# Attention, a wide gated layer and eight experts on one core: a new order for the first phase, and copies by halves where the experts begin

## The chip, the cores and the metric

The kernel runs on one core of a Trainium2 chip. The metric is the device time of one execution in microseconds (us), given as the median of several runs. Of the engines, PE multiplies matrices, DVE and ACT do elementwise work, POOL does the indirect transfers and some small fills, and SP issues almost all other transfers. Each engine works through its own instructions strictly in the order in which they were emitted, so one instruction that waits holds all behind it.

## The reference, cut to what matters

Windowed attention (window 64) feeds a wide layer, and that feeds a top-1 mixture of eight experts; every token is either routed or passed through.

```python
scores = (q @ k.T) / sqrt(64), masked to 0 <= i - j < 64          # 4 x 8 heads, 576 positions, 64 wide
x = softmax(scores) @ v  -> rows of 512                            # 2304 tokens x 512
h = x @ w_in; g = h * tanh(softplus(h)); x = g @ w_out             # 512 -> 2048 -> 512
do = x @ w_skip > 0; e = argmax(x @ w_gate); p = softmax prob of e # router, 8 experts
out = x;  out[do] = x + p * (relu(x @ w1[e]) @ w2[e])              # 512 -> 1024 -> 512
```

## The kernel before, in words

The 2304 tokens are cut into six blocks of 384. In the first phase each block goes through attention (four pairs of heads, `pr`, two units each), then through the wide layer in 16 chunks of 128 hidden columns, chunk `c` being `L1` (into the chunk), an elementwise chain on DVE and ACT, and `L2` (out of it, accumulated over the block in three PSUM tiles `po`). Products are made from a high and a low part of each operand (three matmuls for one), so each weight is loaded (`wl`), put together from its words and split into two parts by DVE and ACT (`we`, `wa`, `wo`, `ws`, `wH`, `wL`) before its first use.

Nothing of this order is written by hand. Each step is a task of a list scheduler (`Plan`, lines 51 to 157): it has one or two engines with a cost, the tasks it comes `after`, the buffers it needs (`get`) and frees (`use`), a due time, and for a transfer a time `lat` from the end of its issue until its data can be used. `order` repeatedly takes, on the engine that can start first, the startable task that is due first; due times are shifted by kind of task (`LATE`), and where two engines could do a task, prices (`PRICE0` up to a planned time `TW0`, then `PRICE`, from `TW` on `PRICE2`) decide. `emit` then issues all tasks in planned order, so each engine's queue is fixed at build time. `T0`, `D0`, `D1`, `US` and `UO` set the planned times of chunks and units.

Where PE has a planned gap, `keep_warm` (line 1163) puts filler matmuls called `warm` into it, as many as fill a share `FILL` = 0.8 of the gap at 0.056 us each. This holds from the start up to the first `L2`, and again from the second routing transpose of the last block on.

In attention, `load_nat` (`lqk`, lines 414 to 427) loads the queries `nq` and keys `nk` of a pair into four shared buffers `rk`; PE transposes them (`nat_T`, `nT`), `kT` and `qT` copy them out of PSUM, `att_S` (`S`) makes the scores, `mx`, `ex`, `ep`, `rc`, `nm` the softmax, `PT` transposes the probabilities, `PV` multiplies by `v`. The scores of pair 2 must come after the `PT` of units 0 and 1, those of pair 3 after the `PT` of units 2 and 3. `lqk` is planned with `lat=2.3`.

The change to the experts, called the handover here, comes after the last chunk. For each of the three tiles `t` of the last block: `xe` copies `po` to `xs`, `rT` transposes it, `re` copies that out, `rl` multiplies by the router's weights, and a chain of tiny DVE steps finds the expert and the slot (`m1`, `su`, `fi`, `m2`, `oh`, then `pl` on PE, then `pi`, `ro`, `ke`); beside it run the gate (`se` on ACT, then `sm`, `ep`, `ga`, `tg`), the slot as an integer (`sl`) and the running count (`co`). `pm` then makes a 0/1 matrix that picks the tile's tokens for expert 0, and `se2` (`select`, line 1096) adds these tokens into two PSUM tiles `sel` by eight matmuls for each `t`: expert 0 so gets its tokens without going through memory. `xgH` copies each `sel` out, and `E1` (line 1217) starts expert 0. `sH` and `sL` split the tokens into parts for `se2`. `eH` and `eL` split weights of the first experts as their places come free.

Of the kernel before, what the change touches and what calls it, by code (L numbers as in the profile page):

```python
# [26 lines left out]
T0, D0, D1, US, UO, WO, LO = 20.57, 3.54, 4.21, 1.68, 5.52, 2.09, 3.4  # L27
# [138 lines left out]
LATE = dict(wl=-9.64, wa=-0.1, wo=-3.47, ws=-4.07, wH=-11.22, lqk=-4.23, nT=-11.43, S=-14.23, ex=-0.53, nm=-4.0, PT=0.94, Pe=7.68, xH=-13.18, L1=2.57, L2=0.89, me=1.15, n=-4.49, mn=-0.61, ln=-5.67, r=-7.61, g=3.04, gH=3.02, xe=2.94, rT=1.62, re=-6.31, rl=2.98, rs=-1.25, lg=13.87, ro=-1.68, eH=16.04, rc=1.8, PV=-0.21, wL=2.42, ga=-3.86, sL=-1.97, xo=13.29, eL=4.54, m2=6.01, bl=18.08, wb=-0.93, ke=-20.26, m1=16.67, se2=-11.46, sl=7.64, el=-0.26, qT=2.69, fz=-9.43, bt=-20.62, se=-13.56, sH=11.09, sd=-1.3, wg=-1.88, tg=9.05, fs=-2.81, xgH=-0.09, sm=9.36, oh=-8.74, su=7.71, xL=-4.21, we=3.45, pl=-8.44, gL=2.75, pi=-2.04, co=-1.2, pm=-0.37, dm=8.62, kT=-2.92, fi=-2.37, mx=3.12, L2t=14.66, ep=-14.67, rq=0.13, lv=-0.43)  # L166
# [5 lines left out]
def tile_kernel(  # L172
# [408 lines left out]
    for pr in range(NU // 2):  # L581
        t = unit_time(2 * pr) - 5
        if pr < NPE:
            T(("lqk", pr), one(SS, 1.8 if len(runs(pr // 4)) == 1 else 2.3), lambda e, pr=pr: load_nat(pr), lat=2.3,
              get=[("rk", ("nq", pr)), ("rk", ("nk", pr))], due=t, t0=.7)
# [249 lines left out]

    def x_store(m, t):
        n = 3 * m + t
        SP.dma_start(out=out[128 * n:128 * n + 128, :], in_=xs_t[m, t][:, :DM])
# [6 lines left out]
    def route_Te(eng, m, t):  # L845
# [5 lines left out]
        xf_t[m, t] = xf  # L851

# [26 lines left out]
    class Group:  # L879


        def __init__(self, m, t0, n):
            self.m, self.t0, self.n, self.i = m, t0, n, 3 * m + t0
# [113 lines left out]
    for m in range(NB):  # L997
# [3 lines left out]
        for t in range(3):  # L1001
            T(("xe", m, t), two(.48, .6), lambda e, m=m, t=t: x_evac(e, m, t), after=[("L2t", NF * m + NF - 1, t) if last else ("L2", NF * m + NF - 1)],
              get=[("xs", ("xs", m, t))], use=[("po", m, t)], due=tb + 2)
            T(("xo", m, t), one(SS, .45), lambda e, m=m, t=t: x_store(m, t), after=[("xe", m, t)], lat=2.5,
              due=tb + 20, use=[("xs", m, t)])
            T(("rT", m, t), one(PP, .43), lambda e, m=m, t=t: route_T(m, t), after=[("xe", m, t)] + [("re", m, t - 1)] * (t > 0),
              get=[("ps", ("rtp", m, t))], due=tb + dt * (2 + 2 * t), use=[("xs", m, t)])
            T(("re", m, t), two(.48, .6), lambda e, m=m, t=t: route_Te(e, m, t), after=[("rT", m, t)],
              get=[("rk" if last else "xf", ("xf", m, t))], use=[("rtp", m, t)])
# [6 lines left out]
            T(("rl", m, t), one(PP, .75), lambda e, m=m, t=t: route_lg(m, t), after=[("re", m, t), ("wg",)],  # L1016
# [5 lines left out]
        prev = None  # L1022
        for t0, n in ([(t, 1) for t in range(3)] if last else [(0, 3)]):
            g = Group(m, t0, n)
# [6 lines left out]
            def R(name, eng, cost, fn, after, use=(), late=0.0, get=(), lat=None, g=g, gb=gb, td=td):  # L1031
# [10 lines left out]
            R("pl", PP, .1, Group.place, [key("oh")] + ([prev("co")] if prev else [("co", m - 1, 0)] if m else []),  # L1042
              get=[("ps", ("pp", m, t0))])
# [8 lines left out]
            R("co", VV, .21 * n, Group.count, [key("pl")], (), 1)  # L1052
# [61 lines left out]
    for t in range(3):  # L1114
        T(("sH", t), two(.52, .34), lambda e, t=t: xs_H(e, t), after=[("xe", L, t)],
          get=[("xHL", "xsHL")] if t == 0 else (), use=[("xs", L, t)], due=te + 10 + t, behind=[("sH", t - 1)] * (t > 0))
        T(("sL", t), one(VV, .6), lambda e, t=t: xs_L(e, t), after=[("sH", t)], use=[("xs", L, t)],
# [6 lines left out]
    for i in range(2):  # L1124
        T(("xgH", i), two(.52, .6), lambda e, i=i: sel_H(e, i), after=[("se2", t, i) for t in range(3)],
          get=[("xHL", "xg0")] if i == 0 else (), use=[("sel", i)], due=te + 16, behind=[("xgH", 0)] * i)
# [6 lines left out]
    for n in range(32):  # L1133
# [8 lines left out]
        T(("eH", key), two(.52, .34), lambda e, key=key, i=i: expert_H(e, key, i), after=[("el", key), last_use[i]],  # L1142
# [21 lines left out]
    def keep_warm(key, t0, t1):  # L1164
# [5 lines left out]
        n = int((t1 - t0 - GAP) * FILL / (0.056 if t0 else 0.085))  # L1170
# [46 lines left out]
    def E1(e, fp):  # L1217
        ph_t[e, fp] = ph = pl1.tile([128, 2, N1], F32, tag="ph2", name="ph2")
        for i in range(2):
            f = 2 * fp + i  # L1220
            for kk in range(NK):
                PE.matmul(ph[:, i], w1_t[e, kk][:, 128 * f:128 * f + 128], xgT[e][:, kk, :N1],  # L1222
                          start=kk == 0, stop=kk == NK - 1)
# [242 lines left out]
```

## Time and profile before

| | us |
|---|---|
| median of 3 runs (lowest, highest) | 687.76 (687.21, 689.37) |
| the profiled execution | 687.16 |
| its span, first to last instruction | 685.4 |
| PE busy in the span | 670.7 |
| DVE busy | 460.1 |
| ACT busy | 405.6 |

PE's busy time holds the fillers too, so a share of 98% doesn't say that it does useful work for 98% of the time. Shares of an engine have to be read stage by stage, since the stages have different limits. A row of the timeline gives the start, the duration, engine, line, operation and output from inputs; a number in square brackets is how long the engine sat idle just before it, with what ended that.

### The profile page before, as it was taken

What the parts mean: (1) busy time and instruction counts of PE and PEld (TensorE: products, weight loads), DVE (VectorE), ACT (ScalarE), POOL (GpSimd) and SP (SyncE); (2) the same over time, 40 slices, a digit from 0 to 9 for tenths busy, and PEclk for the clock granted to TensorE, in tenths of its full rate; (3) what the DMA queues carried; (4) which work ended last, traced back from release to release, by engine and by line L of the source; (5) the groups of instructions that cost most, each with busy time, mean ns of one, the idle gap of its engine ahead of it and who ended that gap; (6) DMA issues with size and microseconds to landing.
All of it is one profiled execution on the core that took longest, in us unless ns stands there. A gap on an engine that the chain in (4) does not pass through costs nothing. (4 is left out here: it accounts for less than half of the span.)

```text
span 685.4 us, 13449 instructions
## 1 busy us (share of the span) xinstructions
PE 670.7 (98%) x4870; PEld 576.7 (84%) x4870; DVE 460.1 (67%) x1298; ACT 405.6 (59%) x994; POOL 55.6 (8%) x114
## 2 busy tenths in 40 slices
PE   8999999999999999999999999999999999999995
PEld 7777767788888888888888888888889888998983
DVE  5999999876665556556776656566678574685352
ACT  5888777677667676676555565455544253543241
POOL 3000000000020001000020001000020122211111
PEclk9999999999999999999999999999999999999998
DMA  9999966776432312232311100044464677578300
GB/s 199 279 316 324 248 134 141 191 162 146 77 75 47 83 35 53 47 93 50 66 44 24 47 1 16 12 153 146 147 200 146 224 251 261 200 286 300 132 27 19
DMA packets 150493, 92.54 MB, mean 135 GB/s; under 512 B 111869, under 2 KB 128253, under 8 KB 150416
## 3 DMA queue, kind: packets, MB, share of 16 engines
q1 hardware_dynamic: 147696, 87.11, 46.5%
q0 software_dynamic: 2720, 4.42, 1.8%
q8 instruction: 46, 0.75, 0.5%
q14 instruction: 31, 0.25, 0.1%
HBM read 73.96 MB, written 17.86 MB: 134 GB/s over the span
## 5 line engine op out<-in xcount | busy, mean ns | idle before, releaser
L737 PE MATMUL ph<-xH,w 128*128 128x384 f32 x768 | 221.1, 349 | 0.1
L788 PE MATMUL po<-w,gH 128*128 128x512 f32 x480 | 154.4, 403 | 0.0
L737 PEld LDWEIGHTS ph<-xH,w 128*128 128x128 f32 x768 | 141.0, 188 | 6.1 <-issue 1.9
L737 PE MATMUL ph<-xL,w 128*128 128x384 f32 x384 | 130.1, 339 | 0.0
L745 ACT ACTIVATE u<-u 128x384 f32<-128x384 f32 x96 | 50.3, 524 | 121.5 <-DVE u L742 121.5
L788 PEld LDWEIGHTS po<-w,gH 128*128 128x128 f32 x480 | 87.3, 189 | 17.1 <-issue 1.6
L788 PE MATMUL po<-w,gL 128*128 128x512 f32 x240 | 95.0, 396 | 0.0
L764 DVE SCALAR_TENSOR_TENSOR u<-u,ph 128x384 f32<-128x384 f32 x80 | 44.1, 551 | 67.7 <-ACT u L758 67.3
L737 PEld LDWEIGHTS ph<-xL,w 128*128 128x128 f32 x384 | 72.3, 188 | 4.4 <-issue 2.6
L1222 PEld LDWEIGHTS ph<-xgT,w 128*128 128x128 f32 x512 | 63.9, 190 | 1.5 <-DVE xgT L319 0.4
L1222 PE MATMUL ph<-xgT,w 128*128 128x144 f32 x512 | 64.7, 287 | 0.4 <-DVE xgT L319 0.3
L742 DVE TENSOR_SCALAR u<-ph 128x384 f32<-128x384 f32 x96 | 53.2, 554 | 15.0 <-PE ph L737 13.8
L773 DVE TENSOR_TENSOR gL<-u,gH 128x384 fp32r<-128x384 f32 x80 | 44.5, 557 | 17.1 <-ACT gH L317 14.2
L531 ACT ACTIVATE P<-P,mx 128x128 f32<-128x128 f32 x144 | 55.8, 391 | 0.3 <-DVE mx L524 0.2
L788 PEld LDWEIGHTS po<-w,gL 128*128 128x128 f32 x240 | 45.1, 188 | 10.7
L749 ACT ACTIVATE u<-u 128x384 f32<-128x384 f32 x96 | 50.4, 525 | 2.9
L755 ACT ACTIVATE u<-u 128x384 f32<-128x384 f32 x96 | 50.2, 523 | 2.3
L758 ACT ACTIVATE u<-u 128x384 f32<-128x384 f32 x96 | 50.2, 523 | 2.3
L788 PE MATMUL po<-w,g 128*128 128x512 f32 x96 | 44.0, 594 | 0.0
L343 DVE TENSOR_TENSOR w<-st,w 128x512 fp32r<-128x512 f32 x64 | 42.6, 683 | 0.6
L1266 PE MATMUL po<-w,hH 128*128 128x512 f32 x128 | 42.6, 414 | 0.0
L1249 ACT ACTIVATE hH<-ph 128x288 fp32r<-128x288 f32 x31 | 12.7, 411 | 42.8 <-PE ph L1222 42.8
(166 smaller groups left out, 965.8 us busy)
## 6 DMA issues: line engine op xcount, KB each, us to landing
st<-in_moe_w_dram SPq DMA_DIRECT2D x64, 256.0 KB, 6.0
w<-in_moe_w_dram SPq DMA_DIRECT2D x32, 512.0 KB, 5.3
w<-in_moe_w_in_dram SPq DMA_DIRECT2D x16, 512.0 KB, 6.4
w<-in_moe_w_out_dram SPq DMA_DIRECT2D x16, 512.0 KB, 6.0
out_dram<-xs SPq DMA_DIRECT2D x18, 256.0 KB, 2.4
xg<-xg_d SPq DMA_DIRECT2D x16, 257.0 KB, 4.5
ca<-w SPq DMA_DIRECT2D x16, 256.0 KB, 3.2
xg_d<-nothing SPq DMA_DIRECT2D x16, 256.0 KB, 4.8
```

The source lines that it names most:

```text
L343: eng.tensor_tensor(l, raw_w.pop(key), h.bitcast(F32), op=ALU.subtract)
L531: A.activation(P[:, i], P[:, i], AF.Exp, bias=mx[:, 0, u % 2, i:i + 1], scale=-1.0, accum_out=mx[:, 1, u % 2, i:i + 1])
L737: PE.matmul(phs[c], a[:, kk], b[:, kk], start=kk == 0 and n == 0, stop=kk == NK - 1 and n == len(terms) - 1)
L742: V.tensor_scalar(u, phs[c], 20.0, None, op0=ALU.min)
L745: A.activation(us[c], us[c], AF.Exp)
L749: A.activation(us[c], us[c], AF.Square, bias=1.0)
L755: A.activation(us[c], us[c], AF.Ln, scale=0.5, bias=half_t[c])
L758: A.activation(us[c], us[c], AF.Exp, scale=-1.0)
L764: V.scalar_tensor_tensor(o, us[c], 1.0, phs[c], op0=ALU.subtract, op1=ALU.mult)
L773: eng.tensor_tensor(gL, us[c], gH.bitcast(F32), op=ALU.subtract)
L788: PE.matmul(po[m, t], a[:, ts], b, start=f == 0 and n == 0, stop=f == NF - 1 and n == len(terms) - 1)
L1222: PE.matmul(ph[:, i], w1_t[e, kk][:, 128 * f:128 * f + 128], xgT[e][:, kk, :N1], start=kk == 0, stop=kk == NK - 1)
```

## The change

**The plan of the first phase.** `lqk` is planned with `lat` 4.8 for pairs 2 and 3 and 2.5 for the others, instead of 2.3 for all. A set of the planner's constants moves: chunk 0 is planned 0.73 earlier, the later attention units 0.62 later in all, `we` and `kT` are due earlier (by 0.90 and 0.61), the prices of the start end at a planned 23.99 instead of 30.94. All tasks of the first phase stay the same, only their order (and, where two engines are possible, the engine) is worked out anew. (Of the `LATE` table the diff below shows the changed entries alone.)

**The handover.** For the last tile (`t` = 2) `xe` and `re` are each done by halves of 256 columns, one on DVE and one on ACT. `pl` of a tile no longer waits for the running count of the tile before, but adds the one-hot rows of the tiles before it by matmuls of its own. `sl`, `sm` and `co` (and with them the gate's chain) come only after the last `pm`. The `sL` of tiles 1 and 2 come after `xe` and `re` of tile 2. The two last expert weights, (2, 5) and (2, 7), are split only after `xgH`. The two `xgH` go to ACT and DVE, one each, and are due 24 earlier. The fillers of this stage fill the whole planned gap instead of 0.8 of it. The first step of `E1` takes the halves of its sum in the order in which the two `xgH` deliver them.

```diff
-T0, D0, D1, US, UO, WO, LO = 20.57, 3.54, 4.21, 1.68, 5.52, 2.09, 3.4
+T0, D0, D1, US, UO, WO, LO = 19.84, 3.52, 4.21, 1.68, 6.87, 2.09, 3.4
-TW0 = 30.94
-PRICE0 = dict(P=0.0, V=2.28, A=0.5, G=-0.5, S=0.0)
-TW = 309.39
-PRICE2 = dict(P=0.0, V=1.26, A=2.91, G=0.0, S=0.0)
+TW0 = 23.99
+PRICE0 = dict(P=0.0, V=2.59, A=0.5, G=-0.5, S=0.0)
+TW = 319.85
+PRICE2 = dict(P=0.0, V=1.11, A=4.08, G=0.0, S=0.0)
...
-LATE: lqk=-4.23, xe=2.94, rT=1.62, rc=1.8, xo=13.29, fz=-9.43, sd=-1.3, xgH=-0.09, we=3.45, co=-1.2, kT=-2.92, fi=-2.37
+LATE: lqk=-3.93, xe=4.36, rT=1.11, rc=1.49, xo=11.62, fz=-9.66, sd=-3.55, xgH=1.14, we=2.55, co=1.72, kT=-3.53, fi=6.04
...
-            T(("lqk", pr), ..., lambda e, pr=pr: load_nat(pr), lat=2.3,
+            T(("lqk", pr), ..., lambda e, pr=pr: load_nat(pr), lat=4.8 if pr in (2, 3) else 2.5,
...
+    def x_evac_half(eng, m, t, n):
+        ...
+        hs = slice(256 * n, 256 * n + 256)
+        if eng is A:
+            A.activation(xs_t[m, t][:, hs], po[m, t][:, hs], AF.Copy, scale=-1.0)
+        else:
+            V.tensor_scalar(xs_t[m, t][:, hs], po[m, t][:, hs], -1.0, None, op0=ALU.mult)
...
+    def route_Te_half(eng, m, t, n):
+        ...
+        copy(eng, xf[:, 2 * n:2 * n + 2], p[:, 2 * n:2 * n + 2])
...
+    def front(self):
+        return self.prev.front + [self.prev.oh[:, 0]] if self.prev else []
...
-                for t2 in range(t):
-                    PE.matmul(pp[:, t], ones8, self.oh[:, t2], start=False, stop=False)
+                for o in self.front + [self.oh[:, t2] for t2 in range(t)]:
+                    PE.matmul(pp[:, t], ones8, o, start=False, stop=False)
...
-            R("pl", ..., [key("oh")] + ([prev("co")] if prev else [("co", m - 1, 0)] if m else []),
+            R("pl", ..., [key("oh")] + ([prev("oh")] if prev else [("co", m - 1, 0)] if m else []),
...
-            R("sl", VV, .07, Group.slot, [key("ro")], (), .5)
+            R("sl", VV, .07, Group.slot, [key("ro")] + [("pm", 2)] * last, (), .5)
+            calm = [("pm", 2)] * last
-            R("sm", VV, .1, Group.sum, [key("se")], (), .5)
+            R("sm", VV, .1, Group.sum, [key("se")] + calm, (), .5)
-            R("co", VV, .21 * n, Group.count, [key("pl")], (), 1)
+            R("co", VV, .21 * n, Group.count, [key("pl")] + calm + ([prev("co")] if prev else []) + [("pl", m, 2)] * last, (), 1)
...
-        T(("sL", t), one(VV, .6), ..., after=[("sH", t)], ...)
+        T(("sL", t), one(VV, .6), ..., after=[("sH", t)] + [("xe", L, 2)] * (t == 1) + [("re", L, 2)] * (t == 2), ...)
...
-        T(("xgH", i), two(.52, .6), ..., due=te + 16, behind=[("xgH", 0)] * i)
+        T(("xgH", i), one(VV if i else AA, .55), ..., due=te - 8, behind=[("xgH", 0)] * i)
...
-        T(("eH", key), two(.52, .34), ..., after=[("el", key), last_use[i]], ...)
+        T(("eH", key), two(.52, .34), ..., after=[("el", key), last_use[i]] + [("xgH", 0), ("xgH", 1)] * (key in ((2, 5), (2, 7))), ...)
...
-        n = int((t1 - t0 - GAP) * FILL / (0.056 if t0 else 0.085))
+        n = int((t1 - t0 - GAP) * (1.0 if stage[0] else FILL) / (0.056 if t0 else 0.085))
...
-            for kk in range(NK):
-                PE.matmul(ph[:, i], ..., start=kk == 0, stop=kk == NK - 1)
+        if e == 0 and fp == 0:
+            order = [(i, kk) for k2 in (0, 2) for i in range(2) for kk in (k2, k2 + 1)]
+        ...
+        for i, kk in order:
+                PE.matmul(ph[:, i], ..., start=(i, kk) == order[0], stop=(i, kk) == order[-1])
```

## Rows read from the trace of the kernel before

**Rows 1.** Windows: start:end, length, busy us (instructions) by engine, clock, DMA share, GB/s.
```profile
6.00:46.00 40.00, 35.58 (x525) 31.27 (x523) 35.16 (x129) 32.29 (x107) 2.35 (x18) 1.00 1.14 268
50.00:110.00 60.00, 60.00 (x373) 42.59 (x373) 59.21 (x153) 47.98 (x120) 1.40 (x6) 1.00 0.88 226
523.90:527.50 3.60, 3.60 (x37) 3.58 (x35) 3.52 (x17) 2.02 (x5) 0.00 (x0) 1.00 0.39 148
527.50:529.50 2.00, 2.00 (x28) 2.00 (x27) 1.72 (x20) 0.21 (x1) 0.00 (x0) 0.60 0.00 0
529.50:532.00 2.50, 2.50 (x18) 2.41 (x16) 2.08 (x19) 0.00 (x0) 0.98 (x1) 0.64 0.03 7
```

**Rows 2.** Windows of the fillers' line alone: length, PE and weight loads, clock, DMA.
```profile
6.00:46.00 40.00, 11.50 (x171) 10.12 (x168) 1.00 1.14 268
523.90:534.32 10.42, 3.19 (x32) 2.65 (x32) 0.84 0.22 83
```

**Rows 3.** Waits of DVE from 6 to 46: total us, times, longest.
```profile
DVE cv L652 <- DMA w<-in_moe_w_in_dram: 1.9, 2, 1.3
DVE cv L652 <- DMA w<-in_moe_w_out_dram: 0.7, 1, 0.7
```

**Rows 4.** Timeline of PE, first phase: pairs 2 and 3.
```profile
13.01 0.52 PE L437 MATMUL tqk<-ident,nq 96*128 96x96 f32 x4 [0.50 <-DMA nq<-in_q_dram]
...
15.37 0.99 PE L552 MATMUL tp<-ident,P 128*128 128x128 f32 x6 [0.89 <-DVE P L547]
...
16.80 1.15 PE L508 MATMUL sc<-kT,qT 64*64 64x128 f32 x24
...
20.36 0.98 PE L552 MATMUL tp<-ident,P 128*128 128x128 f32 x6
...
22.16 0.89 PE L508 MATMUL sc<-kT,qT 64*64 64x128 f32 x24
```

**Rows 5.** Timeline of DVE, first phase.
```profile
14.34 0.43 DVE L652 TENSOR_SCALAR cv<-w 128x512 int32<-128x512 int32 x1 [1.27 <-DMA w<-in_moe_w_in_dram]
```

**Rows 6.** Timeline of SP, first phase.
```profile
7.91 0.85 SPq L425 DMA_DIRECT2D nq<-in_q_dram  x1
```

**Rows 7.** Timeline of PE, handover.
```profile
525.59 1.91 PE L873 MATMUL lp<-wgs,xf 128*128 128x9 f32 x16
...
527.57 1.71 PE L1176 MATMUL warm<-ones 128*128 128x128 bf16 x17
...
529.52 0.56 PE L1099 MATMUL sel<-pick,xsH 128*128 128x256 f32 x1
...
532.44 0.56 PE L1176 MATMUL warm<-ones 128*128 128x128 bf16 x7
532.81 0.37 PE L1099 MATMUL sel<-pick,xsH 128*128 128x256 f32 x1
...
534.32 8.22 PE L1222 MATMUL ph<-xgT,w 128*128 128x144 f32 x64 [0.29 <-DVE xgT L319]
```

**Rows 8.** Timeline of DVE, handover.
```profile
524.95 0.68 DVE L343 TENSOR_TENSOR w<-st,w 128x512 fp32r<-128x512 f32 x1
525.55 0.16 DVE L898 TENSOR_REDUCE r_mx<-lp 128x1 f32<-128x8 f32 x1
...
528.71 0.34 DVE L1093 TENSOR_SCALAR pick<-iota,row_all 128x256 fp32r<-128x256 int16 x1
...
531.35 0.68 DVE L343 TENSOR_TENSOR w<-st,w 128x512 fp32r<-128x512 f32 x1
531.94 0.35 DVE L1093 TENSOR_SCALAR pick<-iota,row_all 128x256 fp32r<-128x256 int16 x1
533.58 1.29 DVE L319 COPY xgT<-sel 128x512 f32<-128x512 f32 x2 [1.29 <-PE sel L1099]
```

**Rows 9.** Groups of ACT by shape: instructions, busy us, mean ns, idle before.
```profile
L317 ACT ACTIVATE kT<-tqk 128x256 f32<-128x256 f32 x2 | 0.8, 378 | 0.2 <-PE tqk L437 0.2
L317 ACT ACTIVATE xf<-rtp 128x512 f32<-128x512 f32 x3 | 1.8, 591 | 5.1 <-PE rtp L843 5.1
```

More of the change, by code (lines that the diff above doesn't have):

```diff
@@ L583, in tile_kernel @@
         if pr < NPE:
-            T(("lqk", pr), one(SS, 1.8 if len(runs(pr // 4)) == 1 else 2.3), lambda e, pr=pr: load_nat(pr), lat=2.3,
+            T(("lqk", pr), one(SS, 1.8 if len(runs(pr // 4)) == 1 else 2.3), lambda e, pr=pr: load_nat(pr), lat=4.8 if pr in (2, 3) else 2.5,
               get=[("rk", ("nq", pr)), ("rk", ("nk", pr))], due=t, t0=.7)
@@ L1001, in tile_kernel @@
         for t in range(3):
-            T(("xe", m, t), two(.48, .6), lambda e, m=m, t=t: x_evac(e, m, t), after=[("L2t", NF * m + NF - 1, t) if last else ("L2", NF * m + NF - 1)],
-              get=[("xs", ("xs", m, t))], use=[("po", m, t)], due=tb + 2)
-            T(("xo", m, t), one(SS, .45), lambda e, m=m, t=t: x_store(m, t), after=[("xe", m, t)], lat=2.5,
+            halves = last and t == 2
+            done = [("L2t", NF * m + NF - 1, t) if last else ("L2", NF * m + NF - 1)]
+            if halves:
+                T(("xe", m, t), one(VV, .3), lambda e, m=m, t=t: x_evac_half(e, m, t, 0), after=done,
+                  get=[("xs", ("xs", m, t))], use=[("po", m, t)], due=tb + 2)
+                T(("xe2", m, t), one(AA, .3), lambda e, m=m, t=t: x_evac_half(e, m, t, 1), after=done,
+                  behind=[("xe", m, t)], use=[("po", m, t)], due=tb + 2)
+            else:
+                T(("xe", m, t), two(.48, .6), lambda e, m=m, t=t: x_evac(e, m, t), after=done,
+                  get=[("xs", ("xs", m, t))], use=[("po", m, t)], due=tb + 2)
@@ L1005, in tile_kernel @@
+            xe = [("xe", m, t)] + [("xe2", m, t)] * halves
+            T(("xo", m, t), one(SS, .45), lambda e, m=m, t=t: x_store(m, t), after=xe, lat=2.5,
               due=tb + 20, use=[("xs", m, t)])
-            T(("rT", m, t), one(PP, .43), lambda e, m=m, t=t: route_T(m, t), after=[("xe", m, t)] + [("re", m, t - 1)] * (t > 0),
+            T(("rT", m, t), one(PP, .43), lambda e, m=m, t=t: route_T(m, t), after=xe + [("re", m, t - 1)] * (t > 0),
               get=[("ps", ("rtp", m, t))], due=tb + dt * (2 + 2 * t), use=[("xs", m, t)])
-            T(("re", m, t), two(.48, .6), lambda e, m=m, t=t: route_Te(e, m, t), after=[("rT", m, t)],
-              get=[("rk" if last else "xf", ("xf", m, t))], use=[("rtp", m, t)])
+            if halves:
+                T(("re", m, t), one(VV, .3), lambda e, m=m, t=t: route_Te_half(e, m, t, 0), after=[("rT", m, t)],
+                  get=[("rk", ("xf", m, t))], use=[("rtp", m, t)])
+                T(("re2", m, t), one(AA, .3), lambda e, m=m, t=t: route_Te_half(e, m, t, 1), after=[("rT", m, t)],
+                  behind=[("re", m, t)], use=[("rtp", m, t)])
+            else:
+                T(("re", m, t), two(.48, .6), lambda e, m=m, t=t: route_Te(e, m, t), after=[("rT", m, t)],
+                  get=[("rk" if last else "xf", ("xf", m, t))], use=[("rtp", m, t)])
@@ L1124, in tile_kernel @@
     for i in range(2):
-        T(("xgH", i), two(.52, .6), lambda e, i=i: sel_H(e, i), after=[("se2", t, i) for t in range(3)],
-          get=[("xHL", "xg0")] if i == 0 else (), use=[("sel", i)], due=te + 16, behind=[("xgH", 0)] * i)
+        T(("xgH", i), one(VV if i else AA, .55), lambda e, i=i: sel_H(e, i), after=[("se2", t, i) for t in range(3)],
+          get=[("xHL", "xg0")] if i == 0 else (), use=[("sel", i)], due=te - 8, behind=[("xgH", 0)] * i)
     last_use = {}
@@ L1218, in E1 @@
         ph_t[e, fp] = ph = pl1.tile([128, 2, N1], F32, tag="ph2", name="ph2")
-        for i in range(2):
+        if e == 0 and fp == 0:
+            order = [(i, kk) for k2 in (0, 2) for i in range(2) for kk in (k2, k2 + 1)]
+        else:
+            order = [(i, kk) for i in range(2) for kk in range(NK)]
+        for i, kk in order:
             f = 2 * fp + i
-            for kk in range(NK):
-                PE.matmul(ph[:, i], w1_t[e, kk][:, 128 * f:128 * f + 128], xgT[e][:, kk, :N1],
-                          start=kk == 0, stop=kk == NK - 1)
+            PE.matmul(ph[:, i], w1_t[e, kk][:, 128 * f:128 * f + 128], xgT[e][:, kk, :N1],
+                      start=(i, kk) == order[0], stop=(i, kk) == order[-1])
     def E1_second(e, fq):
```

31 lines of the change are left out of this document (20 added, 11 removed).

## Prediction, made before the changed kernel was run

> **What bounds the kernel now.** I read the windows first, stage by stage, because PE's 98% counts fillers as work. From 6 to 46 us PE was busy for 35.6 of 40 us and DVE for 35.2 [rows 1], but 11.5 us of PE's time were fillers [rows 2]. So PE did some 24 us of useful work in 40, and the stage is set by DVE, ACT and landings, in a web of short steps. From 50 to 110 PE was busy for all of 60 us, without one filler, and DVE for 59.2 [rows 1]: here PE bounds, with DVE only just ahead of it. After that PE stays full up to the handover, where fillers come back: 3.2 us of the 10.4 between 523.9 and 534.32 [rows 2], at a granted clock of 0.60 and 0.64 from 527.5 to 532 [rows 1]. Since PE is the bound on either side, a microsecond taken out of the start or out of the handover should come off the end, and one gained for DVE or ACT anywhere else is worth nothing. The waits [rows 3] and the timeline [rows 4 to 8] then say what the steps of these two stages wait for.
>
> **The handover, part by part.** The point to move is 534.32, where expert 0 starts [rows 7].
>
> *Halves of the last tile's copies.* They shorten two copies, but from 523.9 to 527.5 PE was busy without a gap [rows 1], and the last 16 router matmuls ran on from 525.59 for 1.9 us [rows 7]. The copies end earlier behind a PE that has other work, so I cost them at nothing. If that cover went, two ACT pieces of 256 columns in parallel would be worth 591 - 378 = 213 ns for one copy [rows 9]. No row here shows DVE and ACT reading one PSUM tile at once. If the halves came one after the other, a copy would take some 2 x 378 = 756 ns for 591, 0.17 us more, again under a busy PE. So: 0, between -0.4 and +0.3 for both copies.
>
> The Trainium skill speaks against this edit: its page "PSUM — Partial Sum Buffer", section Terms, says that two engines must not access the same bank in the same quadrant at once, two reads included. If the halves are kept apart for that reason, it is the +0.17 a copy just worked out, and the sum below would be -2.0 instead of -2.35; no run so far shows it.
>
> *Less on DVE ahead of the picks.* The first router step of tile 0 ran at 525.55, right behind a weight split of 0.68 that had started at 524.95 [rows 8]; it waited for that split if its own inputs were there. The change puts this split behind `xgH`, which brings tile 0's chain forward by up to 0.55. The gate's steps, the integer slot and the count of tiles 0 and 1 (eight tiny steps before the first pick, each holding DVE for about 0.07, estimated from their starts) leave too: 0.56. So the first pick, 528.71 [rows 8], could come up to 1.1 us earlier.
>
> *The selection.* The 16 `se2` matmuls of tiles 0 and 1 ran from 529.52 to 532.44 [rows 7], 2.9 us, behind 17 fillers that began at 527.57 and ran for 1.7 [rows 7]. They had been planned at 0.056 each and took about 0.09, since the clock was 0.60 [rows 1]. How much of the 1.1 arrives depends on these fillers, which PE takes in order and which now fill the whole planned gap (1.25 times as many for one gap, but the gaps get shorter). Ends: nothing earlier, and the full 1.1. I take 0.9, nearer to the upper end, since the weight split alone gives 0.55 and fillers are planned from gaps that the shorter chain closes.
>
> *The last pick.* It ran at 531.94, behind another weight split of 0.68 from 531.35 [rows 8], and its matmuls began at 532.81 after a filler of 0.56 [rows 7]. Without that split, and with `pl` freed from the count, it is ready at about 530.4 (five dependent steps of about 0.2, their spacing in the timeline, after 527.5, then `pl`, three more steps and the pick of 0.35). It then no longer ends last: PE goes from the 16 matmuls straight on, and the 0.37 between 532.44 and 532.81 goes.
>
> *`xgH` by two engines, `E1` reordered.* Both copies ran on DVE, 1.29 together from 533.58 [rows 8]; `E1` started after the first, and waited 0.29 in all [rows 7]. The second copy is hidden by the first matmuls of `E1` before as after. ACT's 591 for 128x512 [rows 9] against DVE's 645 is -0.05; the splits now put behind `xgH` meet idle engines. I add up 0.9 + 0.37 + 0.05 = 1.3, and 0.2 for the clock: the same selects begin sooner after the router's thin matmuls, in a denser stretch. **Handover: -1.5** (E1 at 532.8). Ends: at the full clock the 16 selects would take some 2.9 x 0.64 = 1.9 [rows 1], which makes -2.5; with a quarter more fillers in front of everything, 0.25 x 3.2 = 0.8 [rows 2], against the 0.37 of the last pick and part of the 1.1, about +0.2.
>
> **The first phase.** Nothing is added or taken away; the question is which waits the new order meets. The planner had counted the queries and keys of a pair as usable 2.3 after their issue. The trace: queries of pair 2 issued from 7.91 for 0.85 [rows 6], their transpose at 13.01 after PE had waited 0.50 for them [rows 4], so they landed about 4.2 after the issue's end. 4.8 is near that, so this 0.50 should go. What held the stage longer stood beside it: DVE waited 1.27 for a weight at 14.34 [rows 5] with the normalisation behind it, and PE's `PT` at 15.37 for that [rows 4]. Such waits for weights are 1.9 + 0.7 = 2.6 in this stage [rows 3], and `wl` keeps its 2.3; `we`, due 0.9 earlier, may meet them again. The gain ends at -(2.6 + 0.5) = -3.1.
>
> The other end: planned later, the transposes of pair 2 may be queued on PE behind the `PT` of units 0 and 1, which ran from 15.37 to 16.36 [rows 4]. Transposes until 17.3, two copies of about 0.48 on ACT (384 columns, between the two sizes of [rows 9]), and the scores come at about 18.2 instead of 16.80: +1.4. SP's queue can't make up for it, since pair 2's loads already start as soon as pair 0's buffers are free. No row is nearer to either end, so I take the middle: **-0.85**. The shift of the later attention units (0.62) and of the prices moves work into a stretch in which DVE has 0.8 us free in 60 [rows 1]; I cost it at nothing as long as it stays inside that.
>
> **The sum**: -1.5 - 0.85 = -2.35. The profiled execution took 687.16 (span 685.4 and 1.76 around it) and would come to 684.8; it lies 0.60 under the median of the runs shown, 687.76, so against that I predict **685.4 us**. A measurement of this kernel can tell about 0.3%, 2.06 us, from no change: faster means below 685.7, slower above 689.8.
>
> **The rivals.**
> 1. *The new order doesn't do what its name says*: pair 2's queries no longer hold PE, but the weight at 14.34 does, so the first phase ends where it did. For it: the largest waits of DVE in that stage are for weights, whose `lat` is unchanged [rows 3]. Against it: the due times of all kinds move too. Only the handover counts: 687.76 - 1.5 = 686.3.
> 2. *The handover hands its gain back to PE's clock and fillers.* The selects wait behind fillers at half speed; these are 3.2 us already [rows 2], and the thin router matmuls ahead of the low clock stay. Against it: the split of 0.68 in front of the last pick goes in any case. Then 687.76 - 0.85 = 686.9, or 687.1 with the +0.2.
> 3. *Slower: PE's order in the first phase turns against it.* The place is 13 to 23 us: pair 2's transposes behind the `PT` (+1.4, above), and then the same for pair 3, whose transposes stood before the `PT` at 20.36 with the scores at 22.16 [rows 4]: behind the `PT` they would come at about 23.3, +1.1. It decides from 1.5 upward, where it has eaten the handover's gain; at 2.5 and a handover that gives only half it ends at 687.76 + 2.5 - 0.75 = 689.5. Against it: pair 3's transposes ran well after their data had landed, so 4.8 need not move them, and DVE's idle time could absorb part.
>
> **How the numbers follow.** Forecast (both parts gain) 0.50, own range 683.2 to 687.0; rival 1 0.18; rival 2 0.16; rival 3 0.16. The forecast's range reaches further down than up: some 0.36 of its 0.50 lies below 685.7. Rival 1 adds 0.06 and rival 2 0.03 there: faster 0.45. Rival 3 lies above 689.8 in about half its cases, and a new stall in the stretch from 50 to 110, which I can't price, adds a little: slower 0.10, within 0.3% 0.45. The range for 8 in 10 goes from 682.9, the forecast's low end with little left out below, to 688.6, which takes in rivals 1 and 2 and leaves out most of rival 3.
>
> **What would show each step.** In the profile after: E1's first matmul relative to the end of the last `L2` matmul (523.9 to 534.32 before), near 8.9 us instead of 10.4; no weight split between the router's steps and the last pick; the selects of tile 2 directly behind those of tiles 0 and 1, with no filler between; the window at 0.60 to 0.64 of the clock no longer than before. In the first phase: no wait of PE for `nq` of pair 2, fewer fillers than 11.5 us up to 46, DVE's waits for weights below 2.6. I would be wrong if PE waits between 50 and 110, if the fillers of the handover grow, or if the scores of pair 2 come later than 16.8.

## The result, and the profile after

The changed kernel takes 695.27 us (median of 5 runs, 693.21 to 695.31) against 687.52 for the kernel before beside it (687.13 to 689.37): ratio 1.0094, 95% interval 1.0072 to 1.0115, so 0.94% slower. The forecast was 685.4 and faster; the sign was wrong. The profiled execution took 695.27 with a span of 693.5, 8.1 more than the span before (685.4).

I compared the two traces at four points: the start of the first `L1` matmul of chunk 8, the end of the last `L2` matmul, the start of `E1` and the end of PE's last matmul. The span's 8.1 divide into +3.23 up to the last `L2` (523.90 to 527.13), -1.85 in the handover (10.42 to 8.57) and +6.7 behind `E1`. Behind `E1` only two experts take longer: from `E1` of expert 0 to that of expert 1 it is 19.99 instead of 15.22, from expert 5 to 6 20.44 instead of 18.51.

The waits of PE behind `E1` (total us, times, longest), and DVE's own in front of the second; the first is the view from 534 to 560, the others that from 600 to 640:

```profile
PE tp L1247 <- DMA xg<-xg_d: 3.3, 1, 3.3
...
DVE w L319 <- DMA st<-in_moe_w_dram: 2.6, 2, 1.9
...
PE ph L1264 <- DVE hL L1297: 1.7, 1, 1.7
```

So in front of expert 1 PE stands still because the gathered tokens of expert 1 (`xg`) have not landed. They are read from `xg_d`, which POOL's scatters fill. The timelines of POOL and SP, first of the kernel before:

```profile
530.63 0.98 POOL L279 DMA_INDIRECT xg_d<-xs,r_si  x1 [21.09 <-DVE gate_all L956]
532.32 0.97 POOL L279 DMA_INDIRECT xg_d<-xs,r_si  x1 [0.71 <-DVE pick L1093]
533.59 0.98 POOL L279 DMA_INDIRECT xg_d<-xs,r_si  x1 [0.30 <-issue]
...
536.95 1.37 SPq L333 DMA_DIRECT2D st<-in_moe_w_dram  x3
538.37 2.98 SPq L1200 DMA_DIRECT2D xg<-xg_d  x6
```

then of the changed kernel:

```profile
537.15 1.51 POOL L279 DMA_INDIRECT xg_d<-xs,r_si  x1 [25.71 <-DVE w L319]
538.97 0.97 POOL L279 DMA_INDIRECT xg_d<-xs,r_si  x1 [0.30 <-DVE hL L1297]
540.24 0.97 POOL L279 DMA_INDIRECT xg_d<-xs,r_si  x1 [0.30 <-issue]
...
542.97 1.30 SPq L333 DMA_DIRECT2D st<-in_moe_w_dram  x3
544.31 2.12 SPq L1239 DMA_DIRECT2D xg<-xg_d  x3
```

and waits of SP from 534 to 546 (total us, times, longest), first the longest of the kernel before, then those of the changed kernel:

```profile
SPq L1432 <- DVE level L1159: 10.8, 1, 10.8
...
SPq L1474 <- DVE level L1198: 11.5, 1, 11.5
SPq L333 <- DMA xg_d<-xs,r_si: 2.3, 1, 2.3
```

The last scatter starts 6.65 us later, while `E1` starts 1.38 later; the first load follows the start of the last scatter by 2.73. A scatter needs the slot (`sl`) and the tagged row (`tg`, behind `sm`), which the change put behind the last pick. On DVE of the changed kernel one sees the rest, the steps behind the last pick in their order:

```profile
533.84 0.35 DVE L1132 TENSOR_SCALAR pick<-iota,row_all 128x256 fp32r<-128x256 int16 x1
...
535.52 0.69 DVE L319 COPY xgT<-sel 128x512 f32<-128x512 f32 x1 [0.41 <-PE cp L1188]
...
536.26 0.27 DVE L983 COPY xs<-gate_all 128x1 f32<-128x1 f32 x3
536.45 0.75 DVE L319 CAST w<-st 128x512 fp32r<-128x512 f32 x2
537.12 1.29 DVE L343 TENSOR_TENSOR w<-st,w 128x512 fp32r<-128x512 f32 x2
538.32 0.16 DVE L1190 TENSOR_REDUCE mc<-cp 128x1 f32<-128x8 f32 x1
...
539.83 0.15 DVE L1199 TENSOR_SCALAR folded<-cp 128x8 f32<-128x8 f32 x1
```

The tags of all three tiles end only at 536.5. Then come the two moved weight splits, 2.0 us, and only behind them the chain of `rounds()` (L1190 to L1199), which works out `level`; SP waits for `level` too before it enters the expert phase. In the kernel before this chain ended 1.89 after `E1`'s start, and the first load came 0.74 behind it; here it ended at 4.28, and the scatters came later still.

### The profile page after: what moved, and what is told of

It is laid out like the page before. It is cut to its first block, busy times and chain, and to the rows that moved or that the text cites. A ratio compares the mean times of both kernels' runs of the same rounds, so it can differ in the third digit from the quotient of the medians.

```text
span 693.5 us, 13413 instructions
## 1 busy us (share of the span) xinstructions
PE 673.9 (97%) x4858; PEld 577.9 (83%) x4858; DVE 471.1 (68%) x1322; ACT 399.2 (58%) x972; POOL 60.2 (9%) x114
## 5 line engine op out<-in xcount | busy, mean ns | idle before, releaser
L745 ACT ACTIVATE u<-u 128x384 f32<-128x384 f32 x96 | 50.1, 522 | 87.3 <-DVE u L742 86.8
L755 ACT ACTIVATE u<-u 128x384 f32<-128x384 f32 x96 | 50.3, 524 | 12.1 <-DVE u L751 9.9
L758 ACT ACTIVATE u<-u 128x384 f32<-128x384 f32 x96 | 50.2, 523 | 2.7
L749 ACT ACTIVATE u<-u 128x384 f32<-128x384 f32 x78 | 40.9, 525 | 2.2
L279 POOL DMA_INDIRECT xg_d<-xs,r_si x18 | 18.7, 1036 | 250.2 <-DVE gH L319 75.2
```

Source lines behind the costliest of these rows:

```text
L745: A.activation(us[c], us[c], AF.Exp)
L755: A.activation(us[c], us[c], AF.Ln, scale=0.5, bias=half_t[c])
L758: A.activation(us[c], us[c], AF.Exp, scale=-1.0)
```

## The experiments

Theory S: the late scatters cost the time. Rival P: the new order of the first phase does. Rival E: the two splits behind `xgH` do. The first four kernels take the change apart.

**e1, the handover alone**: the changed kernel with the constants and `lat` of before.

```diff
-lat=4.8 if pr in (2, 3) else 2.5     # and the new T0 ... LATE
+lat=2.3                              # and the old ones
```

> The planner's constants and the landing times of the kernel before, with all edits of the handover. The ledger of the changed kernel against the one before is +3.2 us up to the last L2 matmul, -1.9 from there to the start of expert 0, +6.7 behind it. Theory S (the last block's scatters come late because the slot, the gate and the count wait for the last pick, so the loads of experts 1 and on start late): handover -1.9 and +4.8 to +6.7 behind it, 690.4 to 692.4. Rival P (the loss behind expert 0 hangs on the new order of the first phase): only the handover's -1.9, 685.6.

Measured: 692.42 against 688.62, ratio 1.0057 (1.0036 to 1.0078). PE waited 3.30 for `xg`.

**e2, the plan alone**: the kernel before with the new constants and `lat`.

> The planner's new constants and landing times, with the handover of the kernel before. Theory S: the start costs +3.2 and nothing is lost behind expert 0, 690.7. Rival P: +3.2 and the +6.7 behind expert 0 too, 697.

Measured: 690.6, ratio 1.0035 (1.0013 to 1.0057); no wait for `xg`. So both halves cost, and neither S nor P is all of it.

**e3, the change with the scatters early**:

```diff
-R("sl", ..., [key("ro")] + [("pm", 2)] * last, ...)
+R("sl", ..., [key("ro")], ...)
-calm = [("pm", 2)] * last
+calm = []
```

> The changed kernel, but the slot and the sum of the gate no longer wait for the last pick (the count still comes after all three placements, which it must, since these now add the earlier tiles themselves). Theory S: the last three scatters start within 1 us of where expert 0 starts less 3, loads of expert 1 follow, PE doesn't wait for them: 695.3 less 4.8 to 6.7, 688.6 to 690.5. Rival E (the two weight splits put behind the copies of the selected tokens hold the buffers, so the loads start late whatever the scatters do): 695, with the first weight load of the expert phase still at about 543.

**e4, the same two lines in e1's kernel**:

> All edits of the handover but the late slot and gate, on the constants and landing times of the kernel before. Theory S: the handover's gain without its price, 687.5 less 1.0 to 1.9, 685.6 to 686.5. Rival E: as the handover alone, 690 or more.

Measured: e3 692.79, ratio 1.0065 (1.0037 to 1.0094); e4 690.35, ratio 1.0028 (1.0004 to 1.0052). About 2 us come back, less than theory S forecast, and PE still waits 1.69 and 1.46 for `xg`: something else now comes last. In both it is the chain of `rounds()`, whose last step ends 0.74 before the first load starts. Rival E was nearer in e4: the two splits do hold the load, here through the chain that stands behind them. (The handover of e3 took 11.34, at a mean clock of 0.85, against 8.57 at 1.00 in the changed kernel; in that profile this takes back 2.8 of the 4.3 that are gained behind `E1`.) That gave theory G: the load waits for several gates, and the latest counts.

**e5, e4 with the splits where they had been**:

```diff
-... + [("xgH", 0), ("xgH", 1)] * (key in ((2, 5), (2, 7)))
```

> As the kernel of e4 (handover with the scatters early, plan of the first phase as before), but the splits of the weights (2, 5) and (2, 7) stand again where they stood in the kernel before, not behind the copies of the selected tokens. Theory G (two gates): the first load of the expert phase starts at the later of two times, 0.74 us after the last step of the rounds chain and 2.73 us after the start of the last scatter. Without the two splits the rounds chain ends some 1.9 us after E1's start, as in the kernel before, instead of 4.28; the load then starts within 3.3 us of E1, PE does not wait for the gathered tokens of expert 1 (1.46 in e4), expert 0 to 1 takes 15.2 to 15.5 us instead of 16.76. The handover itself gets longer by the splits in front of the first router step and the last pick, some 0.4 to 0.9. In all about 688.0 to 689.0, 1.0 to 2.0 below e4. Rival E2 (the wait comes from the gathers' own landing under traffic, not from when they are started): expert 0 to 1 stays at 16.5 to 17, and the time at 690 or above.

Measured: 690.7, ratio 1.0033 (1.0020 to 1.0047). A miss. The rounds chain did end at `E1` + 2.0, yet the load started only at `E1` + 4.86 behind the scatters (last one at 535.70, load 3.47 after it), and PE waited 1.82. With the splits back in front of the picks the scatters themselves came late against `E1`.

**e6, e4 with the chain of `rounds()` made a task**, ahead of the splits:

```diff
+T(("rc2",), one(PP, .1), ..., after=[("co", L, 2)], get=[("ps", "cp")], due=te + 12)
+T(("rd",), one(VV, 1.4), lambda e: rounds(), after=[("rc2",)], use=["cp"], due=te + 12)
-... + [("xgH", 0), ("xgH", 1)] * (...)
+... + [("xgH", 0), ("xgH", 1), ("rd",)] * (...)
```

> As the kernel of e4, but the rounds chain stands on DVE directly behind the last count and the last pick, where DVE had been idle for 1.62 us, and the two splits stay behind the copies of the selected tokens. Theory G: the gate by the rounds chain is gone, the gate by the last scatter holds (scatter + 2.73, about 3.0 us after E1's start against 2.6 in the kernel before, with about 1.1 us to spare there). No wait of PE for the gathered tokens of expert 1; expert 0 to 1 takes 15.2 to 15.5. The copy on DVE of the selected tokens may start up to 0.3 later, half hidden behind the first four matmuls. The handover keeps its 8.6 to 8.9 us. In all 687.0 to 688.0, level with the kernel before or better by up to 0.2%. Rival E2: expert 0 to 1 stays at 16.5 to 17 and the time at 690.

Measured: 689.49, ratio 1.0014 (1.0001 to 1.0027); no wait for `xg`, handover 8.74. The wait fell as theory G says; the time stayed 1.3 above the kernel before, which I had not expected.

**e7 and e8, one suspect each in the kernel before**: only `sl` and `sm` behind the last pick (e7), only the two splits behind `xgH` (e8).

> The kernel before with one edit of the change alone: the integer slot and the gate's sum of the last block come only after the last pick. Theory G: the last scatter starts some 3 to 4 us later (after the last pick come the slots, the gate's chain and the tags, then three scatters 1.3 to 1.8 apart), the first load of the expert phase 2.73 after it, so 2.5 to 4 later than in the kernel before, and PE waits for the gathered tokens of expert 1 for that less 1.1: 1.4 to 2.9. Time 689 to 690.5. Rival E2: no wait, 687.5.

> The kernel before with one edit of the change alone: the splits of (2, 5) and (2, 7) behind the copies of the selected tokens. Theory G: the scatters keep their place, the rounds chain ends about 2.0 us later against E1 (3.9 instead of 1.89), the load of the expert phase 0.74 after that, so the wait for the gathered tokens of expert 1 is about 0.9 to 1.0; E1 itself comes up to 0.9 earlier after the last L2. Time 687 to 688: gain and loss nearly even. Rival E2: no wait, and 686.7.

Measured, one execution each, so without a verdict on the time: 689.25 with a wait of 1.33, the load 2.74 after the last scatter; 689.83 with a wait of 1.48, the load 0.74 after the rounds chain. Either edit by itself makes PE wait, each by its own gate.

**e11, the kernel before with the splits behind `xgH` and the chain of `rounds()` ahead of them**, and **e12, the kernel before with the halves alone**:

> The kernel before with two small edits of the handover: the splits of (2, 5) and (2, 7) come behind the copies of the selected tokens, as in the change, but the rounds chain stands ahead of them (directly behind those copies, where it was relative to E1 before). Theory G: E1 starts some 0.8 us earlier after the last L2 (9.6 instead of 10.4), the rounds chain still ends 1.9 us after E1's start, so the load starts 2.6 after E1 and PE does not wait for the gathered tokens; 686.8 to 687.6, 0.1 to 0.2% faster. Rival E2: the splits delay the first low part of the hidden rows on DVE and PE waits there: as before or 0.1% slower.

> The kernel before with the halves of the last tile's two copies alone. In the traces so far the half on ACT began only when the half on DVE had ended (0.04 to 0.07 us after), so a copy takes two halves in a row, 0.42 + 0.39, against 0.59 or 0.69 whole. Theory: the router's matmuls of tile 2 begin up to 0.2 later, hidden in part by the matmuls of tile 1; E1 after the last L2 at 10.4 plus 0 to 0.2, time as before within 0.1%. Rival (the halves are worth something by freeing an engine): E1 0.2 to 0.4 earlier.

Measured: e11 690.25, ratio 1.0031 (1.0017 to 1.0045), a miss: the chain ended 1.9 after `E1`, as wanted, but the load came 3.9 after it. A third gate shows among SP's waits in e11:

```profile
SPq L1440 <- DVE level L1165: 9.9, 1, 9.9
SPq L333 <- DVE w L343: 1.3, 1, 1.3
```

The load goes into the staging buffers that these two splits empty, and it started 0.14 after the second split's end, as the rows of DVE and SP show; in e6 too.

```profile
537.98 1.28 DVE L343 TENSOR_TENSOR w<-st,w 128x512 fp32r<-128x512 f32 x2
...
539.40 1.30 SPq L333 DMA_DIRECT2D st<-in_moe_w_dram  x3
```

e12, a miss too: 691.0, ratio 1.0041 (1.0026 to 1.0057), with no wait for `xg`, but a handover of 10.05 at full clock. DVE's timeline of e12 shows where this comes from: worked out anew, the plan now puts the second weight split, which stood in front of the last pick [rows 8], right behind the first router step, with the first split ahead of it:

```profile
526.05 0.68 DVE L343 TENSOR_TENSOR w<-st,w 128x512 fp32r<-128x512 f32 x1
526.65 0.16 DVE L921 TENSOR_REDUCE r_mx<-lp 128x1 f32<-128x8 f32 x1
526.73 0.68 DVE L343 TENSOR_TENSOR w<-st,w 128x512 fp32r<-128x512 f32 x1
```

So e12 does not price the halves by themselves; e17, below, does. Against the 9.23 that the kernel before needs at full clock (e13, below) this is 0.8 more; the rest of e12's 2.7 us is open.

All profiles together (e13 to e17 are described below), by the start of the first `st` load after `E1`:

| kernel | load after `E1` | gate | PE's wait for `xg` | `E1` to expert 1 |
|---|---|---|---|---|
| before, e9, e10, e12, e13, e14 | 2.62 to 2.64 | rounds | 0 | 15.21 to 15.23 |
| e2 | 2.78 | rounds | 0 | 15.38 |
| e15, e16, e17 | 3.19 to 3.20 | scatter | 0 | 15.10 to 15.11 |
| e6 | 3.43 | split | 0 | 15.60 |
| e11 | 3.90 | split | 0 | 15.42 |
| e7 | 4.65 | scatter | 1.33 | 16.74 |
| e5 | 4.86 | scatter | 1.82 | 18.72 |
| e3, e4 | 5.01, 5.02 | rounds | 1.69, 1.46 | 16.99, 16.76 |
| e8 | 5.16 | rounds | 1.48 | 16.91 |
| e1, after | 7.13, 7.27 | scatter | 3.30, 3.32 | 21.39, 19.99 |

The wait is the start of the load after `E1` less 3.0 (4.86 - 1.82) to 4.0 (7.27 - 3.32), whichever gate makes it; below that it is nothing. The kernel before, at 2.63, had some 0.4 to 1.3 to spare. Each row is one execution; those of e1 and e5 took 694.88 and 694.97, 2.5 and 4.3 above the medians of their kernels, so their last column stands for that execution and not for the kernel.

**e9 and e10, the two parts of the plan**: `lat` alone, constants alone.

> The kernel before with one edit of the change alone: the planner's landing time of the queries and keys (4.8 for pairs 2 and 3, 2.5 for the others), constants as before. In the profiles so far the stretch from the first L1 matmul of chunk 8 to the end of the last L2 was 447.92 to 447.94 us with the old plan and 449.17 to 449.61 with the new one, whatever the ramp did before it. Theory C (the constants make the +1.4, above all the later attention units): 447.9 in this stretch here, and the median within 0.5 of the kernel before. Rival L (the later landings make it): 449.2 and a median of 689.5.

> The kernel before with the planner's constants of the change alone (T0, D0, UO, the prices and their ends, the due times), landing times as before. Theory C: 449.2 or more from chunk 8 to the last L2, with the scores of 24 matmuls taking 1.38 instead of 0.81 us in the stretch between chunks 12 and 16; median 689.5 to 691. Rival L: 447.9 there and a median as before.

Measured: 691.57, ratio 1.0069 (1.0039 to 1.0099), and 692.26, ratio 1.0060 (1.0039 to 1.0082). Both theories fall: from chunk 8 to the last `L2` it is 446.84 and 447.57, not 449.2 in either, and each part alone starts chunk 8 at 80.7 and 80.1 (77.1 to 78.0 with both) and takes more than both together in e2 (though the intervals overlap). The effects of two edits of one plan don't add up.

**e13 and e14, the kernel before itself and with one step more.**

> The kernel before itself, unchanged, as a kernel of its own. Theory N (the rest of 0.1 to 0.4% belongs to the edits): ratio 1.000 within 0.001, chunk 0 starts near 34.5 as in its first profile, 447.93 from chunk 8 to the last L2. Rival V (the start of chunk 0 varies by itself, 34.5 to 37, and the first profile was a quick one): ratio 1.000, but chunk 0 starts at 35 to 37.

> The kernel before with the last step of the rounds chain done twice (0.08 us more on DVE, 1 us inside the slack that the load of the expert phase has). Theory N: ratio 1.000, within 0.001. Rival P2 (any edit of the program's last part costs 0.1 to 0.4%, whatever it does): 689 to 690.5.

Measured: 688.03, ratio 0.9998 (0.9987 to 1.0010), and 688.51, ratio 1.0004 (0.9989 to 1.0018). So a kernel built anew is no slower for that; but rival V holds: in its second profile the kernel before starts chunk 0 at 37.10 instead of 34.47, with the same order, and its handover takes 9.23 instead of 10.42. The windows of e13 in the handover, columns as in [rows 1], the last one the whole handover:

```profile
529.57:531.57 2.00, 1.88 (x31) 1.70 (x29) 1.98 (x25) 0.21 (x1) 0.00 (x0) 1.00 0.00 0
531.57:534.90 3.33, 3.33 (x33) 3.12 (x32) 2.36 (x16) 0.00 (x0) 1.96 (x2) 1.00 0.20 75
525.97:535.20 9.23, 8.81 (x97) 8.40 (x94) 8.15 (x56) 2.23 (x6) 2.25 (x3) 1.00 0.22 85
```

So the clock of 0.60 and 0.64 in [rows 1] comes in some executions and not in others: here the same instructions run at 1.00 throughout, while e14, whose order is the same up to the last step, shows the mean of 0.84 and the 10.42 again.

**e15, the change with both gates open** (e3's and e6's edits together):

> The changed kernel with both gates open: slot and gate no longer wait for the last pick (scatters early), and the rounds chain stands ahead of the two splits as in e6. Theory G plus the first phase: no wait of PE for the gathered tokens, expert 0 to 1 at 15.2 to 15.6, the handover near 8.7, the first phase as in the changed kernel (449.2 to 449.6 from chunk 8 to the last L2): e6 + 1.4 to 2.4, 690.9 to 691.9, some 3.5 to 4.5 below the changed kernel. If another cost sat in the change, it stays at 693 or above.

Measured: 689.71, ratio 1.0028 (1.0015 to 1.0042), no wait for `xg`: 15.11 from expert 0 to 1, a handover of 8.74, 449.20 from chunk 8 to the last `L2`, and a time 1.2 below the range expected. 0.66 of the 0.94% are gone.

**e16, e15 with less on DVE in chunks 12 to 16**:

```diff
-price = self.price or (PRICE0 if now < TW0 else PRICE if now < TW else PRICE2)
+price = self.price or (PRICE0 if now < TW0 else dict(PRICE, V=4.0) if 88 < now < 118 else PRICE if now < TW else PRICE2)
```

> The kernel of e15 (the change with both gates open), with the planner's price of DVE at 4.0 instead of 2.33 between the planned times 88 and 118 alone, so that steps that two engines could do go to ACT there. In 11 executions with the old plan chunks 8 to 16 took 43.32 to 43.33, with DVE busy for 42.7 of them; in four with the new plan 44.08 to 44.41, DVE 43.7. Theory D (the new order brought a microsecond of DVE's work forward into a stretch where DVE had 0.6 to spare, so DVE bounds there): chunks 12 to 16 take 21.3 to 21.4 instead of 22.07, DVE is busy for 20.9 of them, and the last L2 ends 0.5 to 0.8 earlier relative to chunk 8 (448.4 to 448.7 instead of 449.20); the time is 688.9 to 689.4. Rival O (the order of PE's scores between the chunks makes the loss, not DVE's load): chunks 12 to 16 stay at 22.0 to 22.1.

Measured: 689.35, ratio 1.0024 (1.0010 to 1.0038). The windows of chunks 8 to 12, 12 to 16 and the 20 us behind, columns as in [rows 1], first of e13 (the old order):

```profile
78.06:100.09 22.03, 22.03 (x136) 15.71 (x135) 21.67 (x55) 18.33 (x47) 1.05 (x4) 1.00 0.74 162
100.09:121.38 21.29, 21.29 (x129) 14.99 (x127) 21.00 (x57) 15.78 (x39) 0.16 (x1) 1.00 0.64 133
121.38:141.38 20.00, 20.00 (x131) 15.70 (x130) 17.13 (x49) 13.74 (x36) 0.00 (x0) 1.00 0.79 184
```

the same windows of the changed kernel:

```profile
77.96:99.99 22.03, 22.03 (x137) 15.70 (x135) 21.91 (x59) 19.63 (x53) 0.00 (x0) 1.00 0.71 174
99.99:122.04 22.05, 21.91 (x128) 15.20 (x127) 21.74 (x65) 16.40 (x45) 0.74 (x5) 1.00 0.76 129
122.04:142.04 20.00, 20.00 (x131) 15.68 (x130) 15.62 (x46) 13.93 (x37) 0.00 (x0) 1.00 0.75 176
```

and of e16:

```profile
77.39:99.42 22.03, 22.03 (x136) 15.69 (x135) 21.90 (x59) 19.63 (x53) 0.00 (x0) 1.00 0.66 161
99.42:120.91 21.49, 21.49 (x128) 14.94 (x127) 21.27 (x64) 18.34 (x50) 0.74 (x5) 1.00 0.74 132
120.91:140.91 20.00, 20.00 (x131) 15.69 (x130) 13.85 (x41) 15.59 (x39) 0.00 (x0) 1.00 0.79 194
```

With the old order DVE is busy for 42.67 of 43.32, with the new one for 43.65 of 44.08, and has 1.5 less to do right after: its work was brought forward into a stretch with 0.65 to spare. Taking work off DVE there gives back 0.56 of the 0.77 (21.49), theory D, though less than the 21.3 to 21.4 it forecast; 0.26 is lost again later (405.36 instead of 405.10 from chunk 16 to the last `L2`), and the time hardly moves.

**e17, e6 with the last tile's copies whole**:

```diff
-halves = last and t == 2
+halves = False
```

> The kernel of e6 (handover, scatters early, rounds chain ahead of the splits, first phase as before), with the last tile's two copies whole again. In e12 the halves alone had a handover of 10.05 at the full clock, 0.8 more than the kernel before at the full clock in e13 (9.23), and the trace of the changed kernel has a copy by halves at 0.90 against 0.59 to 0.68 whole. Theory H (the halves run one after the other and cost that on the way to the picks): the handover goes from 8.74 to 8.1 to 8.5, and the time from 1.0014 to 0.999 to 1.001. Rival W (the copies are hidden behind PE's matmuls, and e12's 10.05 came from another order of its fillers): the handover stays at 8.7 and the time at 1.001 to 1.002.

Measured: 688.45 against 688.59, ratio 0.9996 (0.9977 to 1.0015), with the handover at 8.78 as against 8.74. The time came where theory H had it, the handover stayed where rival W had it: the halves cost the handover nothing that shows, and the 0.14% of e6 can't be pinned on them, since the two intervals overlap. e17 is level with the kernel before; no kernel here beats it.

## Why the prediction was wrong, point by point

**What was never costed: the gates of the expert phase.** The step that failed is in the part "Less on DVE ahead of the picks" and in the sentence "the splits now put behind `xgH` meet idle engines". I counted what these eight small steps and the splits left behind when they went, not who waits for them at their new place: the scatters on POOL's queue need `sl` and `tg`, the chain of `rounds()` stands behind the splits on DVE, and the splits' own buffers are the next loads' targets. The kernel before had 0.4 to 1.3 us to spare; the change delays the load by 4.64 (7.27 for 2.63). By e15 this is 0.66%, some 4.5 us (the two intervals leave some 1.7 either way), most of the loss. The first two gates could be read from the trace of before, had I followed SP's first load of the expert phase back.

**The first phase, -0.85.** The term was mis-sized and of the wrong sign. In 12 profiles with the old order chunk 8 started at 75.96 to 78.06 (mean 77.17), in four with the new one at 77.09 to 77.96 (77.39): the ramp gained nothing. Rival 1 was right for it: pair 2's queries no longer hold PE, whose transpose of `nq` at 14.01 follows without a wait, but DVE still waited 2.5 for a weight in the changed kernel (2.6 in [rows 3], 2.9 in e13), and PE 1.59 in front of `PT` at 16.09 (0.89 in [rows 4], 2.55 in e13). PE's rows of the changed kernel, and under them DVE's wait from 6 to 46:

```profile
13.62 0.55 PE L437 MATMUL tqk<-ident,nk 96*128 96x96 f32 x4
14.01 0.49 PE L437 MATMUL tqk<-ident,nq 96*128 96x96 f32 x4
16.09 0.88 PE L552 MATMUL tp<-ident,P 128*128 128x128 f32 x6 [1.59 <-DVE P L547]
...
17.42 2.18 PE L508 MATMUL sc<-kT,qT 64*64 64x128 f32 x24 [0.23 <-ACT P L531]
...
DVE cv L652 <- DMA w<-in_moe_w_in_dram: 2.5, 1, 2.5
```

So the 0.50 went, as forecast, and on the mean of the 12 and the four profiles the scores of pair 2 came at 18.19 and 17.65. It was lost again at pair 3, whose scores came at 23.89 and 25.08: the first `PV` and the second `PT`, both ahead of them, ran at 24.83 and 25.68 in the changed kernel and at 17.88 and 20.36 before. At chunk 0 the two orders are level, 36.03 and 35.81. Most of the signs I had named for this phase could not tell, since the kernel before passes them too: in e13 its scores of pair 2 come at 19.31 (17.42 after, 16.80 in [rows 4]), and its fillers up to 46 take 12.07 (12.10 after, 11.50 in [rows 2]). What I had put at nothing, "as long as it stays inside" DVE's 0.8 free in 60, did not stay inside: 44.08 to 44.41 for chunks 8 to 16 in place of 43.32 to 43.33, then 404.92 to 405.51 to the last `L2` in place of 404.59 to 404.62. PE, which I had wanted busy from 50 to 110, now stands still for 0.14 there. Together +1.6 on the mean end of `L2` (525.10 and 526.72); for 0.56 of the 0.77 in chunks 12 to 16 e16 shows the cause, for the rest no run does.

**The handover, -1.5.** Measured against [rows 7] it is 10.42 to 8.57, -1.85, and most signs came: no split ahead of the last pick (which came 6.71 after the last `L2` instead of 8.04), fillers from 3.19 [rows 2] to 1.82, no low clock in this execution (e3, with the same handover but for slot and gate, had it). But the old handover at full clock needs 9.23 (e13) and 9.33 (e2), so the edits are worth about 0.7; the rest was the clock of one execution, of which I had taken 0.2. The first pick came only 0.43 earlier (4.38 instead of 4.81 after `L2`), not 0.9 to 1.1. I had not followed the `sL`, nor the half of `re` that moves from ACT to DVE: before, the `sL` of tile 1 started ahead of the end of `L2` (523.90) and only that of tile 2 behind it; in the changed kernel (`L2` ends at 527.13, first pick at 531.51) both stand ahead of the first pick. DVE's rows, first of the kernel before:

```profile
523.74 0.69 DVE L1084 TENSOR_TENSOR xsL<-xs,xsH 128x512 fp32r<-128x512 f32 x1
...
526.11 0.68 DVE L1084 TENSOR_TENSOR xsL<-xs,xsH 128x512 fp32r<-128x512 f32 x1
```

then of the changed kernel:

```profile
527.51 0.68 DVE L1123 TENSOR_TENSOR xsL<-xs,xsH 128x512 fp32r<-128x512 f32 x1
...
528.89 0.42 DVE L319 COPY xf<-rtp 128x256 f32<-128x256 f32 x1
...
529.31 0.69 DVE L1123 TENSOR_TENSOR xsL<-xs,xsH 128x512 fp32r<-128x512 f32 x1
```

By the starts of DVE's steps, an estimate: the split (0.60), the shorter `xe` (0.26) and the eight steps (0.56) go, one `sL` (0.60) and the half of `re` (0.34) come, and 0.48 is left. And four fillers of 0.40 together still stood in front of the last selects, so only part of the 0.37 went.

*The halves.* They came one after the other, as ACT's row of the changed kernel says, with DVE's half ahead of it:

```profile
527.17 0.42 DVE L844 TENSOR_SCALAR xs<-po 128x256 f32<-128x256 f32 x1 [0.23 <-PE po L788]
...
527.68 0.39 ACT L842 ACTIVATE xs<-po 128x256 f32<-128x256 f32 x1 [1.31 <-DVE xs L844]
```

That is 0.90 for a copy of 0.59 or 0.68, more than the loss of 0.17 I had put as the upper bound; but the cover I named held (e17), so the value taken, 0, was right. The Trainium skill's rule ("PSUM — Partial Sum Buffer", Terms) is not tested by it: ACT waited for DVE's half by a semaphore of the program, so these rows do not have both engines on `po` at once. Both halves also write the same tile `xs`; which of the two tiles made the program keep them apart is open.

**The rivals.** The result lies on rival 3's side, slower, but not by its mechanism: pair 2's transposes stayed ahead of the `PT`, and so did pair 3's (20.68 and 25.68). The rival that was missing is the late gate.

**The expert phase's second wait.** Late loads stay late: 70 us on, the loads of the changed kernel still start 5 to 6 us later against `E1` than before. In e1, e5, e8 and after PE waits 0.9 to 2.4 in expert 5 for DVE's `hL`, which stands behind DVE's waits for staged weights (`st`); in e4 and e7 it waits less than 0.4. PE's wait is what DVE had waited less 0.9 to 1.0: 0.2 of 1.2 in e3, 0.9 of 1.8 in e1, 1.7 of 2.6 in after, 2.4 of 3.3 in e5, and none of 1.0 in e13, the kernel before. Why the weights come late in one and not the other is open. So is the rest of e6 and e11 (0.1 and 0.3% with the first phase in the old order and no wait for `xg`): from `E1` to PE's last matmul they take 143.6 and 143.8 against 142.5 to 142.9 in before, e13 and e14, which covers part of it.

## What to carry to other kernels

When a step is moved behind the critical point, follow everything that hangs on it to the next phase's first loads, on every queue, and note the slack of each gate; the latest gate sets the phase, and opening one only shows the next. In a stretch where two engines are both nearly full, work brought forward is not free, however small the idle share looks elsewhere. Profile the unchanged kernel twice before taking a low clock or a landing wait of one execution for a property of the kernel.

## What the runs showed of the hardware

- The same program starts its first wide-layer chunk at 34.47 in one execution and at 37.10 in another: the weight that DVE waits for near 15 us landed 5.51 after the start of its issue in the first and 7.22 in the second (DVE's wait for it was 1.3 and 2.9), and in the second the granted clock was at its lower level (0.5, 1.2 GHz) from 16.04 to 22.87, beginning while PE waited 2.55 for `P`.
- The clock of the handover fell in some executions and not in others of the same order (mean 0.84 before and in e14, 1.00 in e13), worth about 1.2 us of 10.4. In the profile before it fell at 527.89, although PE was busy for all of 523.90 to 529.50 [rows 1], with the router's matmuls just ahead [rows 7].
- PE's clock after the wait for `xg` was lower where it had stood longer: in the 5 us behind waits of 1.33, 1.46, 1.48 and 1.69 it was 1.00 (2.4 GHz), behind waits of 1.82, 3.30 and 3.32 its mean was 0.66, 0.50 and 0.71. From `E1` to expert 1 the two waits of 3.3 went with 4.8 (after) and 6.2 us (e1) more than the 15.22 before.
- The first load behind a scatter started 2.73 to 2.74 us after the start of the last scatter in after, e1, e7, e15, e16 and e17, and 3.47 in e5. A load behind the `rounds()` chain started 0.73 to 0.74 after the chain's last step (before, e2, e3, e4, e8, e9, e10, e12, e13).
